# Routing tokens to experts: rows of x written straight to the experts' order, with token number and gate, instead of a routing table in DRAM

## The chip, the cores and the metric

The kernel runs on one core of a Trainium2 chip. The metric is the device time of one execution in microseconds (us). The core has five engines that run side by side, each with its own in-order list of instructions: TensorE (PE; its weight loads are PEld), VectorE (DVE), ScalarE (ACT), GpSimd (POOL) and SyncE (SP), which here only issues DMAs. TensorE has two clock levels, 1.2 and 2.4 GHz; the profile gives the granted clock as a share of full speed.

## The reference

```python
def _attn_ref(r, k, v, w, u):                 # batch 4, 8 heads, 768 steps, head size 48
    for t in range(S):
        cur = einsum('bhd,bhe->bhde', u * kt, vt)
        y[:, :, t] = einsum('bhd,bhde->bhe', rt, state + cur)
        state = w * state + einsum('bhd,bhe->bhde', kt, vt)

def _moe_ref(x, w_gate, w1, w2, capacity):    # 3072 tokens x 384, 8 experts of 384 -> 1024 -> 384
    expert_idx = argmax(x @ w_gate, axis=1)
    gate_w = softmax(x @ w_gate)[arange(N), expert_idx]
    # each expert takes its tokens in token order, at most capacity (768) of them
    h = maximum(einsum('ecd,edf->ecf', disp, w1), 0)
    y = einsum('ecf,efd->ecd', h, w2)
    out[i] = gate_w[i] * y[expert_idx[i], pos[i]]      # kept tokens, the others are zero
```

The output of the attention, with the heads side by side, is the x of the experts.

## The kernel before

**Attention loop.** The 3072 tokens are 24 tiles of 128. The loop over the tiles is written out as a hand-made software pipeline: iteration i issues, in this order, the loads of tile i+5 (`load`, on SP's and ACT's queues), the bonus products of tile i+3 (`bonus`, two GpSimd products), the scores of tile i+1 (`scores` on TensorE, `masks` on VectorE), the diagonals of tile i+2 (`diag`, ACT), the back projection of tile i-1 (`back_out`), then `values` and `update` of tile i on TensorE, a step of the routing (`advance`), `prep_keys`, the state update (`state_of`) and `prep_values` (its `reduce_bonus`, L450, is the VectorE sum that waits for the bonus products), and at its end up to two routing scatters (`scatters(2)`). Each engine runs its own share of that order.

**Routing.** `back_out` turns the attention result of a tile into token-major x in PSUM, together with the gate logits; ACT copies x to SBUF (L505) and SP writes it to the DRAM tensor `x_dr` (L506). Tiles are routed in groups of four, at the end of two: `route` finds each token's expert, adds to the running counts per lane (`lane`, L105, on GpSimd but for the last group), ranks the tokens by two small matmuls (L112 and L113), and makes a `slot` (expert * 3072 + rank) and a gate per token. The pair (token number, gate) of each token stands in `pay`. An indirect DMA per tile (`scatters`, L133) writes 128 pairs of 8 bytes to the DRAM table `tbl` at their slots. In iteration 2 GpSimd has filled that table with a number out of bounds.

**Experts.** There are nine passes: expert 0 twice (its first 160 places, then 256 more), each other expert once with 416 places. Before a pass SP reads the pass's part of the table back into `ids` (`table`, L213), and GpSimd gathers the rows of x by the token numbers in it with four indirect DMAs (`gather`, L222); numbers out of bounds are skipped. Then come the transposes (`xtrans`, L231), two layers of fp32 products in three parts each (`layer1`, `layer2`), transposes back and a scatter to the output (`finish`, `emit`, L283 and L275), scaled by the gate from `ids`.

**The order around the change.** Pass 0 needs tokens of the first 16 tiles only: its table is read at iteration 19 and its rows are gathered at iterations 21 and 22 (two gathers each, called a to d in the prediction) from the first 2048 rows of `x_dr`, beside the loop. After the loop come its transposes, the back projection and routing of the last tile, layer 1, the last scatters, and after four blocks of layer 1 the tables of pass 1 and of all later passes and the gathers of passes 1 and 2. From pass 1 on the gather of pass k+2 is issued at the start of pass k. Scatters among themselves are declared independent; any other pair of a write and a read of the same DRAM tensor by indirect DMA is ordered by a wait.

Of the kernel before, what the change touches and what calls it, by code (L numbers as in the profile page):

```python
# [18 lines left out]
C = 128  # L19
NC = S // C  # L20
NI = B * NC
# [4 lines left out]
OOB = 1 << 30  # L26
# [8 lines left out]
def rwkv_moe(nc, tc, dmj, rkv, bdc, wv, uv, ub, wg, w1, w2, out, cap):  # L35
# [4 lines left out]
    with ExitStack() as ctx:  # L40
# [3 lines left out]
        tbl = dram.tile([E * NT, 2], I32, name="tbl")  # L44
# [6 lines left out]
        pay = const.tile([128, NI, 2], I32, name="pay")  # L51
        oob = const.tile([128, E * NT * 2 // 128], I32, name="oob")
# [17 lines left out]
        def back(i, xs, sm, ps1, nd=None):  # L70
            gi, i0, n = grp[i]
            if i == i0:
                lsum[gi] = sm.tile([128, n, E], F32, tag="l", name=f"l{gi}")
            xp = ps1.tile([128, NP, 96 + E], F32, tag="xp", name=f"xp{i}")
            for p in range(NP):
                nc.tensor.matmul(xp[:, p], lhsT=xs[:, p], rhs=sel[:, p], start=True, stop=True)
            nc.vector.tensor_reduce(out=lsum[gi][:, i - i0], in_=xp[:, :, 96:].rearrange("p a e -> p e a"), axis=AX.X, op=ALU.add)
            if i == i0 + n - 1:
                routing.append(route(gi, i0, n, lsum.pop(gi), sm, ps1, nd))
            return xp  # L80
# [7 lines left out]
        def route(gi, i0, n, l, sm, ps1, nd):  # L88
# [37 lines left out]
            nc.vector.reciprocal(out=pay[:, i0:i0 + n, 1].bitcast(F32), in_=zs)  # L126
            todo.extend((i, nd) for i in range(i0, i0 + n))
# [3 lines left out]
        def scatters(n):  # L131
            for i, nd in todo[:n]:
# [6 lines left out]
        def flags(sm, ps1):  # L139
# [4 lines left out]
            cs = sm.tile([128, E + 2], F32, tag="cs", name="cs")  # L144
            nc.vector.tensor_copy(out=cs, in_=ct)
            ff = sm.tile([128, E + 4], F32, tag="ff", name="ff")
# [14 lines left out]
        with ExitStack() as mc:  # L161
# [9 lines left out]
            xg = [keep.tile([WL // 4, 4, DM], F32, name=f"xg{j}") for j in range(2)]  # L171
# [36 lines left out]
            def table(k, rows):  # L208
                e, s0, _, _ = PASSES[k]
                q = max(PASSES[j][2] for j in rows)  # L210
                n = len(rows)
                t = keep.tile([q, n, 4, 2], I32, name=f"ids{k}")
                nc.sync.dma_start(out=t.rearrange("p e i t -> p e (i t)"),  # L213
                                  in_=tbl.rearrange("(e n) t -> e (n t)", e=E)[e:e + n, 2 * s0:2 * s0 + 8 * q]
                                  .rearrange("e (p k) -> p e k", k=8))
                for j, kk_ in enumerate(rows):
                    ids[kk_] = t[:, j]

            def gather(k, n=NT, part=range(4)):
# [52 lines left out]
            def emit(k, i, yp, qo):  # L272
                yo = mo.tile([qo, DM], F32, tag="yo", name=f"yo{k}_{i}")
                nc.scalar.mul(out=yo, in_=yp, mul=ids[k][:qo, i, 1:2].bitcast(F32))  # L274
                r = nc.gpsimd.indirect_dma_start(out=out[:, :], out_offset=bass.IndirectOffsetOnAxis(ap=ids[k][:qo, i, 0:1], axis=0),  # L275
# [30 lines left out]
            sb = [wk.tile([128, 2, NP, 128], F32, name=f"s{j}", bufs=1) for j in range(3)]  # L306
            snb = [wk.tile([128, NP, 64], F32, name=f"snb{j}", bufs=1) for j in range(2)]
# [55 lines left out]
            def setup3():  # L363
# [17 lines left out]
            wz = oob.bitcast(BF16)[:, 0:512]  # L381
# [160 lines left out]
            for i in range(NI):  # L542
# [33 lines left out]
            yt = buf.tile([128, 3, WL], F32, name="yt")  # L576
            for j in range(3):
# [9 lines left out]
            scatters(NI)  # L587
            act()
# [14 lines left out]
            table(1, [1])  # L603
            table(2, list(range(2, len(PASSES))))
# [222 lines left out]
```

## Time and profile before

| | us |
|---|---|
| median of 3 runs | 454.87 |
| lowest and highest | 452.69, 457.9 |
| profiled execution | 453.87 |
| its span, first to last instruction | 452.1 |
| TensorE busy in the span | 390.6 (86%) |
| VectorE, ScalarE, GpSimd busy | 257.6, 201.3, 184.8 |

The profile gives for each engine how long it was busy, for each line of the kernel how long its instructions took and what ended the idle time before them (`[4.42 <-POOL lane L105]`: idle for 4.42 us until GpSimd's instruction of line 105 was done), and for each DMA the time from issue to landing. A busy engine in one stage says nothing of another: the loop over the tiles ends near 172 us, the passes over the experts follow.

### The profile page before, as it was taken

To read this page: it belongs to the slowest core of one execution; us is meant where nothing else is said; L and a number is where in the kernel's file an instruction comes from. 1 tells how busy PE (TensorE), PEld (TensorE's weight loads), DVE (VectorE), ACT (ScalarE), POOL (GpSimd) and SP (SyncE) were. 2 spreads that over 40 slices of the span, in tenths; PEclk is the share of its full clock that TensorE was granted. 3 is DMA by queue.
4 is the path that set the end of the run, shared out by engine and by line. 5 is a ranking of instruction groups with operands and counts; after the bars stand their busy time and mean duration, and the time that the engine had idled before them with its cause. 6 is when DMAs were issued, how large, how long until landed. Compare 5 with 4: busy or idle time off the path is not lost.

```text
span 452.1 us, 8646 instructions
## 1 busy us (share of the span) xinstructions
PE 390.6 (86%) x3234; PEld 364.9 (81%) x3235; DVE 257.6 (57%) x527; ACT 201.3 (45%) x502; POOL 184.8 (41%) x224
## 2 busy tenths in 40 slices
PE   4599868798977587949999999999999999999950
PEld 1489657687866477939999999999999999999940
DVE  6799897887687354815545464553654545543100
ACT  2577546575453233516455273462643634524020
POOL 5765784978366352247440330423303301103030
PEclk8589997896798858987999999999999999999995
DMA  8899999999996252863734553554545534301020
GB/s 220 227 237 280 289 139 219 183 188 216 156 246 108 29 99 45 100 178 111 220 105 132 158 150 123 158 154 146 151 127 170 160 96 129 112 0 50 2 61 1
DMA packets 24871, 64.18 MB, mean 142 GB/s; under 512 B 6575, under 2 KB 9991, under 8 KB 24821
## 3 DMA queue, kind: packets, MB, share of 16 engines
q1 hardware_dynamic: 18101, 49.01, 43.8%
q0 software_dynamic: 5184, 9.82, 8.0%
q10 hardware_dynamic: 1536, 4.72, 5.5%
q8 instruction: 27, 0.44, 0.5%
q14 instruction: 23, 0.19, 0.2%
HBM read 54.26 MB, written 10.05 MB: 142 GB/s over the span
## 4 chain that ended last, share of the span: by engine, by line
PE 30%; issue 20%; POOL 4%; DMA 1%; POOLq 0%
PE a L250 5%; PE a L248 5%; PE a L249 5%; PE b L267 4%; PE b L269 4%; PE b L268 4%; POOL out L275 3%; PE yp L283 2%; PE tp L231 1%; POOL xg L222 1%; DMA xg<-x_dr,ids 1%; DMA tbl<-pay,slot 0%; POOLq L771 0%; POOLq L275 0%; POOLq L222 0%
## 5 line engine op out<-in xcount | busy, mean ns | idle before, releaser
L427 ACT ACTIVATE s<-eye,bon 128x128 f32<-128x128 f32 x192 | 58.7, 388 | 58.2 <-DVE bon L450 57.6
L275 POOL DMA_INDIRECT out<-yo,ids x36 | 36.0, 1001 | 105.2 <-ACT yo L274 104.0
L248 PE MATMUL a<-xh,ws 128*128 128x416 f32 (+1 forms) x216 | 76.8, 355 | 0.0
L249 PE MATMUL a<-xl,ws 128*128 128x416 f32 (+1 forms) x216 | 73.8, 342 | 0.0
L250 PE MATMUL a<-xh,ws 128*128 128x416 f32 (+1 forms) x216 | 73.8, 341 | 0.0
L267 PE MATMUL b<-hh,ws 128*128 128x416 f32 (+2 forms) x216 | 73.3, 339 | 0.0
L269 PE MATMUL b<-hh,ws 128*128 128x416 f32 (+2 forms) x216 | 71.6, 331 | 0.0
L268 PE MATMUL b<-hl,ws 128*128 128x416 f32 (+2 forms) x216 | 71.3, 330 | 0.0
L222 POOL DMA_INDIRECT xg<-x_dr,ids x36 | 38.0, 1056 | 79.5 <-PE tp L231 57.5
L195 DVE TENSOR_TENSOR ws<-wr,ws 128x384 fp32r<-128x384 f32 (+1 forms) x110 | 66.3, 620 | 6.9 <-ACT ws L193 6.7
L254 DVE SCALAR_TENSOR_TENSOR hl<-a,hh 128x416 fp32r<-128x416 f32 (+1 forms) x72 | 39.8, 553 | 51.0 <-ACT hh L253 50.7
L253 ACT ACTIVATE hh<-a 128x416 fp32r<-128x416 f32 (+1 forms) x72 | 35.2, 489 | 73.6 <-PE a L250 73.3
L193 ACT CAST ws<-wr 128x384 fp32r<-128x384 f32 (+1 forms) x112 | 59.8, 556 | 6.0 <-DMA wr<-w 6.0
L270 DVE COPY yt<-b 128x416 f32<-128x416 f32 (+2 forms) x27 | 14.6, 542 | 66.3 <-PE b L269 66.3
L458 PEld LDWEIGHTS a<-dm 48*128 48x128 f32 x384 | 27.6, 214 | 20.7 <-DVE s L462 12.7
L458 PE MATMUL a<-dm 48*128 48x128 f32 x384 | 32.9, 314 | 13.0 <-DVE s L462 7.2
L248 PEld LDWEIGHTS a<-xh,ws 128*128 128x128 f32 x216 | 42.3, 196 | 0.5
L249 PEld LDWEIGHTS a<-xl,ws 128*128 128x128 f32 x216 | 42.2, 195 | 0.3
L250 PEld LDWEIGHTS a<-xh,ws 128*128 128x128 f32 x216 | 42.0, 195 | 0.2
L268 PEld LDWEIGHTS b<-hl,ws 128*128 128x128 f32 x216 | 40.7, 189 | 0.3
L267 PEld LDWEIGHTS b<-hh,ws 128*128 128x128 f32 x216 | 40.7, 189 | 0.2
L269 PEld LDWEIGHTS b<-hh,ws 128*128 128x128 f32 x216 | 40.5, 188 | 0.3
(133 smaller groups left out, 614.1 us busy)
## 6 DMA issues: line engine op xcount, KB each, us to landing
bd<-bdc SPq DMA_DIRECT2D x24, 576.0 KB, 8.0
wr<-w SPq DMA_DIRECT2D x24, 512.0 KB, 5.2
wr<-w SPq DMA_DIRECT2D x32, 384.0 KB, 3.4
dm<-dmj ACTq DMA_DIRECT2D x24, 192.0 KB, 9.0
dm<-dmj SPq DMA_DIRECT2D x24, 192.0 KB, 6.5
x_dr<-x SPq DMA_DIRECT2D x24, 192.0 KB, 5.4
xg<-x_dr,ids POOLq DMA_INDIRECT x36, 4.3
out<-yo,ids POOLq DMA_INDIRECT x36, 4.1
```

The source lines that it names most:

```text
L193: nc.scalar.copy(out=hi, in_=r)
L195: eng.tensor_tensor(out=lo, in0=r, in1=hi.bitcast(F32), op=ALU.subtract)
L222: nc.gpsimd.indirect_dma_start(out=xg[k % 2][:q, i], out_offset=None, in_=x_dr[:n, :], in_offset=bass.IndirectOffsetOnAxis(ap=ids[k][:q, i ...
L248: nc.tensor.matmul(a, lhsT=wh, rhs=xh[:, d, :n], start=d == 0, stop=False)
L249: nc.tensor.matmul(a, lhsT=wh, rhs=xl[:, d, :n], start=False, stop=False)
L250: nc.tensor.matmul(a, lhsT=wl, rhs=xh[:, d, :n], start=False, stop=d == 2)
L267: nc.tensor.matmul(o, lhsT=wh, rhs=hh[:, f, :n], start=f == 0, stop=False)
L268: nc.tensor.matmul(o, lhsT=wh, rhs=hl[:, f, :n], start=False, stop=False)
L269: nc.tensor.matmul(o, lhsT=wl, rhs=hh[:, f, :n], start=False, stop=f == 7)
L275: r = nc.gpsimd.indirect_dma_start(out=out[:, :], out_offset=bass.IndirectOffsetOnAxis(ap=ids[k][:qo, i, 0:1], axis=0), in_=yo, in_offset= ...
L427: nc.scalar.mul(out=s[:, h, p], in_=eye, mul=t["bon"][:, 2 * p + h:2 * p + h + 1])
L458: nc.tensor.matmul(a[:, h, p], lhsT=t["dm"][r, 1, p], rhs=t["dm"][r, 0, p], start=True, stop=True)
```

## The change

Each tile's row of x, 384 numbers, gets two more columns, the token number (as a float) and the gate, in a row of 400 (1600 bytes). The scatter writes that whole row at the token's slot of a new DRAM tensor `xsd`, already in the experts' order. The write of x to `x_dr` by SP, the table, its fill and its read-back fall away. Three row buffers `xr` of four tiles each stand in SBUF.

Where an expert's rows lie is then known without a table: place p of an expert is read if p lies below the expert's end, which is the count of its tokens. `counts` (the count matmuls that the flags needed anyway) is moved ahead, and `places` makes from it a penalty and an index for each place of all later passes; `early_places` does so for pass 0 from the counts after 16 tiles. `gather` reads by these indices; `take` then turns the two extra columns of the gathered rows into output indices and gates, ahead of each pass's transposes. The gather of pass 1 now follows the last scatters directly. The branches that run only for unusual inputs are rewritten to match (left out below).

```diff
@@ back: the copy of x goes into the row buffer
+            xr = rows(gi)
             if i == i0:
                 lsum[gi] = sm.tile([128, n, E], F32, tag="l", name=f"l{gi}")
+                nc.scalar.copy(out=xr[:, 0:n, DM], in_=idf[:, i0:i0 + n])
...
-            return xp
+            nc.scalar.copy(out=xr[:, i - i0, 0:DM].rearrange("p (a b) -> p a b", a=NP), in_=xp[:, :, 0:96])
@@ route, scatters
-            nc.vector.reciprocal(out=pay[:, i0:i0 + n, 1].bitcast(F32), in_=zs)
-            todo.extend((i, nd) for i in range(i0, i0 + n))
+            nc.vector.reciprocal(out=xr[:, 0:n, DM + 1], in_=zs)
+            todo.extend((i, xr[:, i - i0], nd) for i in range(i0, i0 + n))
...
-                r = nc.gpsimd.indirect_dma_start(out=tbl[:, :], out_offset=bass.IndirectOffsetOnAxis(ap=slot[:, i:i + 1], axis=0),
-                                                 in_=pay[:, i], in_offset=None, bounds_check=E * NT - 1, oob_is_err=False)
+                r = nc.gpsimd.indirect_dma_start(out=xsd[:, :], out_offset=bass.IndirectOffsetOnAxis(ap=slot[:, i:i + 1], axis=0),
+                                                 in_=row.bitcast(I32), in_offset=None, bounds_check=E * NT - 1, oob_is_err=False)
@@ new
+        def places(k, n, end, sm):
+            sh = [128, n, 4]
...
+            nc.vector.tensor_tensor(out=pen[:, k:k + n], in0=pos[:, k:k + n], in1=end.unsqueeze(2).broadcast_to(sh), op=ALU.is_ge)
+            nc.vector.scalar_tensor_tensor(out=pidx[:, k:k + n], in0=pen[:, k:k + n], scalar=FAR, in1=pos[:, k:k + n],
+                                           op0=ALU.mult, op1=ALU.add)
+
+        def early_places(sm, ps1):
+            ct = ps1.tile([128, 1], F32, tag="lg", name="ct0")
+            nc.tensor.matmul(ct, lhsT=ones, rhs=lane[:, SNAP, 0:1], start=True, stop=True)
+            places(0, 1, ct, sm)
@@ table falls away; gather, take
-                    nc.gpsimd.indirect_dma_start(out=xg[k % 2][:q, i], out_offset=None, in_=x_dr[:n, :],
-                                                 in_offset=bass.IndirectOffsetOnAxis(ap=ids[k][:q, i, 0:1], axis=0),
-                                                 bounds_check=n - 1, oob_is_err=False)
+                    nc.gpsimd.indirect_dma_start(out=xg[k % 2][:q, i].bitcast(I32), out_offset=None, in_=xsd[:, :],
+                                                 in_offset=bass.IndirectOffsetOnAxis(ap=pidx[:q, k, i:i + 1], axis=0),
+                                                 bounds_check=E * NT - 1, oob_is_err=False)
+
+            def take(k):
+                q = PASSES[k][2]
+                t = keep.tile([WL // 4, 4], I32, tag="ids", name=f"ids{k}", bufs=2)
+                g = keep.tile([WL // 4, 4], F32, tag="gw", name=f"gw{k}", bufs=2)
+                nc.vector.scalar_tensor_tensor(out=t[:q], in0=pen[:q, k], scalar=FAR, in1=xg[k % 2][:q, :, DM], op0=ALU.mult, op1=ALU.add)
+                nc.vector.tensor_copy(out=g[:q], in_=xg[k % 2][:q, :, DM + 1])
+                ids[k] = t, g
@@ setup on GpSimd
-                nc.gpsimd.iota(pay[:, :, 0], pattern=[[C, NI]], base=0, channel_multiplier=1)
-
-            def setup4():
-                nc.gpsimd.memset(oob, OOB)
-                nc.gpsimd.dma_start(out=tbl.rearrange("(p n) t -> p (n t)", p=128), in_=oob)
+                ii = sup.tile([128, NI], I32, name="ii")
+                nc.gpsimd.iota(ii, pattern=[[C, NI]], base=0, channel_multiplier=1)
+                nc.gpsimd.tensor_copy(out=idf, in_=ii)
+                ip = sup.tile([128, len(PASSES), 4], I32, name="ip")
+                for k, (e, s0, _, q) in enumerate(PASSES):
+                    nc.gpsimd.iota(ip[:, k], pattern=[[q, 4]], base=e * NT + s0, channel_multiplier=1)
+                nc.gpsimd.tensor_copy(out=pos, in_=ip)
+                for t in xrb:
+                    nc.gpsimd.memset(t[:, :, DM:], 0.0)
@@ back_out
-                xp = back(i, T[i]["xs"], sm, ps1, "tbl")
-                x = wk.tile([128, DM], F32, tag="x", name=f"x{i}")
-                nc.scalar.copy(out=x.rearrange("p (a b) -> p a b", a=NP), in_=xp[:, :, 0:96])
-                nc.sync.dma_start(out=x_dr[C * i:C * i + C, :], in_=x)
+                back(i, T[i]["xs"], sm, ps1, lambda g: xrb[g % 3], "rows")
@@ the loop over the tiles
                 if i == 19:
-                    table(0, [0])
+                    early_places(sm, ps1)
                 if i in (21, 22):
-                    gather(0, C * SNAP, ((0, 1), (2, 3))[i - 21])
-                if i == 2:
-                    setup4()
+                    gather(0, ((0, 1), (2, 3))[i - 21])
@@ after the loop
+            take(0)
             for j in range(3):
                 xtrans(0, j)()
...
             scatters(NI)
+            counts(ps1)
+            places(1, E, cs[:, 0:E], sm)
+            gather(1)
             act()
...
-            table(1, [1])
-            table(2, list(range(2, len(PASSES))))
-            gather(1)
             gather(2)
...
+            take(1)
             for d in range(3):
                 xtrans(1, d)()
...
                 if k + 1 < len(PASSES):
+                    take(k + 1)
```

## Rows read from the trace of the kernel before

**Rows 1.** The busy time of each engine by stage: the stretch in us, its length, then busy us (and instructions) of PE, PEld, DVE, ACT and POOL, the granted TensorE clock as a share of full speed, the DMA engines' busy share, and GB/s.

```profile
140.00:160.00 20.00, 12.38 (x184) 10.91 (x184) 10.45 (x30) 7.58 (x25) 8.41 (x10) 0.84 0.38 41
...
180.00:200.00 20.00, 15.69 (x134) 15.27 (x132) 11.82 (x37) 7.51 (x19) 6.00 (x7) 1.00 0.77 145
200.00:210.00 10.00, 7.36 (x37) 6.41 (x37) 2.39 (x5) 3.16 (x7) 7.83 (x8) 0.50 0.29 85
...
220.00:437.00 217.00, 215.69 (x1257) 210.73 (x1256) 101.79 (x186) 92.29 (x192) 52.85 (x52) 1.00 0.40 118
```

**Rows 2.** The chain of waits that ended last, in order of time: start, us, what.

```profile
183.66 0.97 DMA tbl<-pay,slot
184.64 12.37 issue
...
201.01 2.68 DMA xg<-x_dr,ids
203.73 1.22 PE tp L231 x9
```

**Rows 3.** The timeline of TensorE, 140 to 210 us: start, us, line, operation, output and inputs, shapes, count, and in brackets the idle time before it and what ended that.

```profile
148.06 1.16 PE L458 MATMUL a<-dm 48*128 48x128 f32 x16
...
157.99 0.17 PE L113 MATMUL rk<-lane,ones 128*128 128x16 bf16 x1 [4.42 <-POOL lane L105]
159.64 2.08 PE L458 MATMUL a<-dm 48*128 48x128 f32 x16 [1.48 <-DVE s L462]
...
174.56 0.94 PE L231 MATMUL tp<-idn,xg 64*128 64x64 f32 x10 [2.30 <-DMA xg<-x_dr,ids]
...
195.41 0.28 PE L269 MATMUL b<-hh,ws 128*128 128x256 f32 x1
200.63 0.37 PE L231 MATMUL tp<-idn,xg 64*128 64x64 f32 x1 [4.94 <-DMA xg<-x_dr,ids]
...
203.73 1.22 PE L231 MATMUL tp<-idn,xg 64*128 64x64 f32 x9 [0.86 <-DMA xg<-x_dr,ids]
```

**Rows 4.** The timeline of SP's DMA queue in the same stretch: the two times at which the routing table is read back.

```profile
149.58 0.54 SPq L213 DMA_DIRECT2D ids<-tbl  x1
...
192.17 1.15 SPq L213 DMA_DIRECT2D ids<-tbl  x2
```

**Rows 5.** The timeline of GpSimd, 140 to 205 us; an indirect DMA's time here is that of its issue, not of its landing.

```profile
153.38 1.01 POOL L133 DMA_INDIRECT tbl<-pay,slot  x1 [10.05 <-DMA ids<-tbl]
...
167.89 0.96 POOL L222 DMA_INDIRECT xg<-x_dr,ids  x1 [0.30 <-issue]
...
183.66 0.97 POOL L133 DMA_INDIRECT tbl<-pay,slot  x1 [0.30 <-issue]
197.22 0.97 POOL L222 DMA_INDIRECT xg<-x_dr,ids  x1 [12.59 <-issue]
...
201.01 0.94 POOL L222 DMA_INDIRECT xg<-x_dr,ids  x1 [0.30 <-issue]
```

**Rows 6.** The timeline of VectorE in the same stretch: the last instruction of a group's gates (L126) and one long wait.

```profile
143.66 0.17 DVE L126 RECIPROCAL pay<-zs 128x2 f32<-128x2 f32 x1
...
157.81 0.55 DVE L450 TENSOR_REDUCE bon<-t 128x8 f32<-128x384 f32 x1 [7.02 <-POOL t L420]
...
162.24 0.17 DVE L126 RECIPROCAL pay<-zs 128x2 f32<-128x2 f32 x1
```

**Rows 7.** Lines of the kernel that issue DMAs: the routing scatter (L133), the final scatter (L275) and the write of x (L506), each with the time of an issue in ns (min/median/max) and, in the row below it, the time from issue to landing of that line's DMAs; the last row is the landing of the gathers (L222).

```profile
L133 POOL DMA_INDIRECT tbl<-pay,slot x24: 975/1002/2344, 52.1 to 183.7; - x24
...
DMA to landing us min/median/max: 6.7/13.9/17.6
L275 POOL DMA_INDIRECT out<-yo,ids x36: 906/996/1314, 207.8 to 436.7; - x36
...
DMA to landing us min/median/max: 2.8/4.1/5.0
L506 SPq DMA_DIRECT2D x_dr<-x x24: 332/347/739, 30.9 to 177.8; - x24
...
DMA to landing us min/median/max: 2.6/5.4/14.2
DMA to landing us min/median/max: 3.2/4.3/5.3
```

**Rows 8.** The busy time by stretches of 4 us in the loop, columns as in rows 1: one in which the first routing scatters are only being issued (from 52) and two that follow the issue of such scatters (from 60 and from 112).

```profile
52.00:56.00 4.00, 3.45 (x64) 3.05 (x65) 4.00 (x6) 2.13 (x8) 3.61 (x3) 1.00 1.04 303
...
60.00:64.00 4.00, 3.04 (x48) 2.55 (x44) 3.96 (x4) 3.33 (x10) 3.70 (x3) 1.00 0.90 81
...
112.00:116.00 4.00, 4.00 (x33) 3.47 (x34) 2.10 (x3) 1.24 (x4) 1.49 (x2) 0.50 0.86 77
```

**Rows 9.** Of the timeline of GpSimd the first bonus product and one that waited for a load, and of ACT's one of its shortest instructions; then of the lists of waits between 20 and 140 us one of GpSimd and the first of VectorE (who waited for whom: us in total, times, longest).

```profile
9.87 1.15 POOL L419 TENSOR_TENSOR t<-bd,ubt 128x384 f32<-128x384 f32 x1 [3.91 <-DMA bd<-bdc]
...
31.51 1.37 POOL L419 TENSOR_TENSOR t<-bd,ubt 128x384 f32<-128x384 f32 x1 [3.10 <-DMA bd<-bdc]
...
161.59 0.22 ACT L109 ACTIVATE z<-z 128x16 f32<-128x16 f32 x1
...
POOL t L419 <- DMA bd<-bdc: 8.1, 3, 3.1
...
DVE ws L195 <- ACT ws L193: 4.9, 4, 3.4
```

More of the change, by code (lines that the diff above doesn't have):

```diff
@@ L43, in rwkv_moe @@
         x_dr = dram.tile([NT, DM], F32, name="x_dr")
-        tbl = dram.tile([E * NT, 2], I32, name="tbl")
+        xsd = dram.tile([E * NT, XW], I32, name="xsd")
+        ebd = dram.tile([2, E], F32, name="ebd")
         idn = const.tile([128, 128], F32, name="idn")
@@ L143, in flags @@
             nc.tensor.matmul(ct[:, E + 1:], lhsT=ones, rhs=lane[:, SNAP, 0:1], start=True, stop=True)
-            cs = sm.tile([128, E + 2], F32, tag="cs", name="cs")
             nc.vector.tensor_copy(out=cs, in_=ct)
+        def places(k, n, end, sm):
+            sh = [128, n, 4]
+            if clamp:
+                c = sm.tile([128, n], F32, tag="cl", name=f"cl{k}")
+                nc.vector.tensor_tensor(out=c, in0=end, in1=top[:, 0:n], op=ALU.min)
+                end = c
+            nc.vector.tensor_tensor(out=pen[:, k:k + n], in0=pos[:, k:k + n], in1=end.unsqueeze(2).broadcast_to(sh), op=ALU.is_ge)
[5 more added lines that the diff above has]
+            places(0, 1, ct, sm)
+        def flags(sm):
             ff = sm.tile([128, E + 4], F32, tag="ff", name="ff")
@@ L170, in rwkv_moe @@
             mc.enter_context(tc.manual_schedule())
-            xg = [keep.tile([WL // 4, 4, DM], F32, name=f"xg{j}") for j in range(2)]
+            xg = [keep.tile([WL // 4, 4, XW], F32, name=f"xg{j}") for j in range(2)]
             wtiles = {}
@@ L206, in rwkv_moe, with gather @@
             ids = {}
[L208 to L219, printed above, removed]
+            def gather(k, part=range(4)):
                 q = PASSES[k][2]
                 for i in part:
-                    nc.gpsimd.indirect_dma_start(out=xg[k % 2][:q, i], out_offset=None, in_=x_dr[:n, :],
-                                                 in_offset=bass.IndirectOffsetOnAxis(ap=ids[k][:q, i, 0:1], axis=0),
-                                                 bounds_check=n - 1, oob_is_err=False)
+                    nc.gpsimd.indirect_dma_start(out=xg[k % 2][:q, i].bitcast(I32), out_offset=None, in_=xsd[:, :],
[8 more added lines that the diff above has]
+                ids[k] = t, g
             def xtrans(k, j):
@@ L306, in rwkv_moe @@
             sb = [wk.tile([128, 2, NP, 128], F32, name=f"s{j}", bufs=1) for j in range(3)]
+            xrb = [wk.tile([128, 4, XW], F32, name=f"xr{j}", bufs=1) for j in range(3)]
             snb = [wk.tile([128, NP, 64], F32, name=f"snb{j}", bufs=1) for j in range(2)]
@@ L380, in rwkv_moe @@
                 nc.sync.dma_start(out=wp[64 * h:64 * h + D], in_=wv[D * h:D * h + D])
-            wz = oob.bitcast(BF16)[:, 0:512]
+            wz = sup.tile([128, 512], BF16, name="wz")
             nc.vector.memset(wz, 0.0)
@@ L687, in reroute, with row_tile @@
         def reroute():
-            nc.gpsimd.dma_start(out=tbl.rearrange("(p n) t -> p (n t)", p=128), in_=oob)
             with tc.tile_pool(name="rw", bufs=2) as rw, tc.tile_pool(name="rs", bufs=2) as rs, \
                     tc.tile_pool(name="rp", bufs=1, space=PSUM) as rp:
+                rows = {}
+                def row_tile(g):
+                    if g not in rows:
+                        rows[g] = rw.tile([128, 4, XW], F32, tag="xr", name=f"rr{g}")
+                        nc.vector.memset(rows[g], 0.0)
+                    return rows[g]
                 for i in range(NI):
@@ L699, in reroute, with ends @@
                     nc.scalar.copy(out=xs, in_=tp)
-                    back(i, xs, rs, rp)
+                    back(i, xs, rs, rp, row_tile)
                     advance()
                     advance()
-                scatters(NI)
-                flags(rs, rp)
+                    scatters(NI)
+                counts(rp)
+                flags(rs)
+                ends()
+        def ends():
+            nc.sync.dma_start(out=ebd[0:1], in_=top[0:1])
+            nc.sync.dma_start(out=ebd[1:2], in_=cs[0:1, 0:E])
         def window(e, s0, n):
@@ L708, in window @@
             with tc.tile_pool(name="vw", bufs=1) as vw, tc.tile_pool(name="vp", bufs=2, space=PSUM) as vp:
-                di = vw.tile([q, 4, 2], I32, name="di")
-                nc.sync.dma_start(out=di.rearrange("p i t -> p (i t)"),
-                                  in_=tbl.rearrange("(e n) t -> e (n t)", e=E)[bass.ds(e, 1), 2 * s0:2 * (s0 + n)]
-                                  .rearrange("o (p k) -> (o p) k", k=8))
+                eb = vw.tile([q, 2], F32, name="eb")
+                for j in range(2):
+                    nc.sync.dma_start(out=eb[:, j:j + 1], in_=ebd[j:j + 1, bass.ds(e, 1)].broadcast_to([q, 1]))
+                wi = vw.tile([q, 4], I32, name="wi")
+                nc.gpsimd.iota(wi, pattern=[[q, 4]], base=s0 - min(cap, NT), channel_multiplier=1)
+                wp_ = vw.tile([q, 4], F32, name="wp_")
+                nc.vector.tensor_copy(out=wp_, in_=wi)
+                nc.vector.tensor_scalar(out=wp_, in0=wp_, scalar1=eb[:, 0:1], scalar2=None, op0=ALU.add)
+                en = vw.tile([q, 1], F32, name="en")
+                nc.vector.tensor_tensor(out=en, in0=eb[:, 0:1], in1=eb[:, 1:2], op=ALU.min)
+                wn = vw.tile([q, 4], F32, name="wn")
+                nc.vector.tensor_scalar(out=wn, in0=wp_, scalar1=en, scalar2=FAR, op0=ALU.is_ge, op1=ALU.mult)
+                nc.vector.tensor_tensor(out=wi, in0=wn, in1=wp_, op=ALU.add)
                 a1 = vw.tile([128, 3, F], F32, name="a1_")
```

46 lines of the change are left out of this document (25 added, 21 removed).

## The prediction, made before the changed kernel was run

> **What bounds the kernel now.** Read the stages first [rows 1]. From 220 us on TensorE is busy 215.69 of 217.00 us at granted clock 1.00: nothing but TensorE work counts there, and the change takes none of it away. Before that there are holes: TensorE works only 15.69 of 20 us in 180 to 200, and 7.36 of 10 us at clock 0.50 in 200 to 210. The chain of waits names the second hole [rows 2]: the last routing scatter is issued at 183.66, a nameless 12.37 us follow, then come the gather of pass 1 and its transposes at 203.73. TensorE's own line agrees [rows 3]: its last matmul of pass 0 starts at 195.41, the transposes wait 4.94 us and again piecemeal until 203.73, and the next matmuls run slow until 210. SP's line says what the 12.37 us are [rows 4]: the read-back of the routing table is issued only at 192.17, when the scatter of 183.66 has landed, 8.5 us after its issue; the gather follows at 197.22 [rows 5], after one more DMA trip.
>
> GpSimd's line shows a first hole [rows 5]. The scatter of tile 16 was ready at about 143.8, when DVE had its gates [rows 6], but started at 153.38 after 10.05 us of waiting: it may not overwrite the table while SP's read of it, issued at 149.58 [rows 4], is under way. Queued behind it is the bonus of tile 23, so DVE stands 7.02 us for it [rows 6], and TensorE 4.42 us for the lane sums behind that [rows 3]. TensorE then runs at 0.50: sixteen score matmuls take 2.08 us at 159.64 against 1.16 at 148.06 [rows 3].
>
> The profiled execution has 452.1 us of span and 453.87 in all; the shown runs have a median of 454.87 (452.69 to 457.9). I sum against 453.87, so the forecast may sit 1 us low against the median.
>
> **The unknown: how long a scatter of whole rows takes to land (L).** After the change every gather waits for the scatters ahead of it, so L sets the result. 8-byte rows took 6.7/13.9/17.6 us (min/median/max); scatters of 1536-byte rows from the same queue at the end of a pass 2.8/4.1/5.0; plain writes of x 2.6/5.4/14.2 [rows 7]. Slow landing goes with tiny rows, not with load alone: where such scatters are in flight the DMA engines are as busy (shares 0.90, 0.86) but move 81 and 77 GB/s, against a share of 1.04 and 303 GB/s just as the first of them are issued [rows 8]. The new rows are 1600 bytes, nearest to the out scatter in queue, operation and size, and nearest to the x write in bytes (128 rows). I take 4.5, between 4.1 and 5.4, and keep 2.8 and 13.9 as ends. The Trainium skill (DMA: Bandwidth & Descriptors, "Anatomy of one DMA") gives about 2.0 us plus bytes over 436 GB/s, an estimate of 2.5 us for 205 KB; the steps below would then end near 434. No row for such a transfer is that short on average, so I stay with the rows.
>
> **First hole.** The table read goes; at iteration 19 stand one small matmul and two DVE operations instead (0.17 us each, as the short ones in [rows 6]). So scatters 16 and 17 go at 144.0 and 145.3 (1.3 apart, as the gathers from 197.22 to 201.01 [rows 5]), the bonus follows, DVE does not stand, and its gates of tiles 18 and 19 come at 155.7 instead of 162.4 (7.02 less, some of it lost to the small operations). TensorE asked for the data of the transposes of pass 0 at 172.3 (174.56 less its wait of 2.30 [rows 3]). Less 7.0, and less 0.9 for each of some three groups of matmuls that ran at 0.50 as the one at 159.64 did, it now asks at about 162.7. But those need gathers that now sit in one queue with scatters and wait for them in both directions, since both touch the same DRAM tensor:
> - scatter 17 lands at 145.3 + 4.5 = 149.8; gathers a and b go at 149.8 and 151.1, land (4.3 [rows 7]) at 155.4;
> - scatters 18 and 19 need that and their gates: 155.7 and 157.0; land at 161.5;
> - gathers c and d: 161.5 and 162.8; land at 167.1.
> Before, gather d was issued at 167.89 [rows 5] and the transposes resumed at 174.56 [rows 3]. So the transposes are 7.4 us earlier; 4.4 of the 11.8 us that TensorE had won turn into a new wait. What GpSimd holds behind those waits, the lane sums of tiles 20 and 21, comes near 159, before TensorE asks at 162.6.
>
> **Second hole.** Scatter 23 went 9.1 us after the transposes (183.66 against 174.56), so now at 176.2, and lands at 180.7. Counts and indices (three matmuls, three DVE operations of 0.17) are ready before, under that landing; should a landing of 2.8 not cover them, they cost 0.5. Four gathers at 180.7 to 184.5 (at the same spacing); the last took 2.7 us then [rows 2], at the median 4.3: landed by 187.2 to 188.8. TensorE ends pass 0 at 195.7 - 7.4 = 188.3. So the transposes of pass 1, whose last part started at 203.73, start at 188.8: 14.9 us gained in all, the 7.4 among them, and almost no wait left. Without the long idle time the 5.2 us from 204.9 to 210.1 at 0.50 [rows 1, 3] become 2.6: another 2.6.
>
> **The rest.** 24 x writes leave SP's queue, where each waited for ACT's copy; the weight and input loads behind them can only go earlier. The fill of the table leaves GpSimd. About 14 short index operations join its setup, at most 2 us, while its first bonus product waits 3.91 us for a load [rows 9]: free, and up to 2 us if that load came at once. ACT gets 8 short copies (the shortest ACT row is 0.22 [rows 9]), and each pass two DVE operations ahead of its transposes. In the last stage DVE is busy 101.79 of 217.00 us [rows 1]; they wait for a gather issued a whole pass earlier, so TensorE does not see them. I charge 0.5 for all this. Moving 4.7 MB from SP's hardware queue to GpSimd's costs GpSimd no more issues: 24 before, 24 after, 1002 ns each at the median [rows 7].
>
> **Sum.** 14.9 + 2.6 - 0.5 = 17.0; 453.87 - 17.0 = 436.9, so 437.
>
> **Rivals.**
> 1. *The landing is set by the software queue, not by row size.* Then L stays at 8.5, as seen from 183.66 to 192.17, or somewhat above. For L above 4.8 each link lengthens: gather d lands at 157.8 + 2L, scatter 23 goes at 166.9 + 2L, pass 1 is there at 173.7 + 3L. L = 8.5 gives 199.2, a gain of 4.5: 449.4; at L = 10.0 nothing is gained: 454. The change would then not shorten what it sets out to. For it: the scatters of tiny and of long rows have 128 rows each, and some issues stretch to 2344 ns [rows 7]. Against it: the out scatters, at 104 rows, are never above 5.0. The Trainium skill (SBUF — State Buffer, "SBUF: two separate sides") warns that DMAs issued from GpSimd wait for descriptors while DVE holds a shared port, which speaks against moving x there; of it this trace shows that stretch of issue time alone. Chance 0.13.
> 2. *Slower: the two-way waits become the bound.* The same chain at L = 13.9, the median of the tiny scatters, puts pass 1 at 215.4, 11.7 later than 203.7: 466. It decides from L = 10.0 on; below that the trip to the table costs more. For it: x writes themselves reached 14.2 under load. Against it: that load is the loop's, and after 140 the DMA share falls to 0.38 [rows 1]. Chance 0.07.
> 3. *The loop gets faster too.* If loads pace it, freeing the DMA engines of tiny rows pays before 140. GpSimd waits 8.1 us for loads between 20 and 140 [rows 9], 3.10 of it at 31.51, before the first scatter; the other 5.0 on top of the sum give 432, and with TensorE's clock kept up in the loop perhaps 428. Against it: DVE's waits there, the longest group of which is 4.9 us behind ACT's weight casts [rows 9], name no load. Chance 0.15.
>
> **How the numbers follow.** The forecast has 0.65: its own spread is L = 2.8 to 6.7, 435 to 444 (at 2.8 TensorE's own work sets the start of pass 1, at 186.6; at 6.7 pass 1 is there at 193.8, a gain of 9.9). The range adds rival 3 below and half of the way to rival 1 above: 428 to 448; it leaves out rivals 1 and 2, 0.20. A measurement of this kernel can tell about 1%, 4.5 us. Faster by over 1%: forecast and rival 3, 0.80. Within 1%: rival 1, 0.13. Slower: rival 2, 0.07.
>
> **What would show it.** In the changed kernel's rows: scatters of whole rows landing in 4 to 5 us; no GpSimd wait of 10 us near 143 and no 7 us wait of DVE; a GpSimd wait of some 4 us ahead of gathers a and c; TensorE's wait at the transposes of pass 0 grown from 2.3 to about 4 us, that of pass 1 shrunk from 8 to under 2; clock 1.00 after it; the span from the last transpose of pass 1 to the end unchanged near 247 us but for the clock. The prediction falls if scatters land in over 7 us, if the loop before 140 changes by more than 3 us either way, or if some wait of the new row buffers shows up in ACT.

## The result and the profile after

The changed kernel takes 435.72 us (median of 4 runs, 434.58 to 439.62) against 455.5 us for the kernel before (median of 4 runs): a ratio of 0.9583 [0.9501, 0.9665], 4.2% faster, where 437.0 was forecast. The profiled execution took 436.04 us, with a span of 434.3 us against 452.1: 17.8 us less, where the sum gave 17.0.

The busy time by stage of the changed kernel, columns as in [rows 1]:

```profile
140.00:160.00 20.00, 16.39 (x208) 14.55 (x209) 15.13 (x41) 8.18 (x25) 10.33 (x13) 0.83 0.16 54
160.00:180.00 20.00, 18.18 (x159) 17.10 (x159) 13.13 (x54) 9.82 (x26) 8.50 (x9) 0.91 0.44 145
180.00:200.00 20.00, 18.74 (x152) 18.32 (x151) 12.01 (x26) 10.12 (x26) 15.43 (x16) 0.91 0.54 160
200.00:210.00 10.00, 10.00 (x86) 9.99 (x85) 4.72 (x12) 2.72 (x7) 3.77 (x4) 1.00 0.61 206
```

The two holes are filled: TensorE works 16.39 us of 140 to 160 (12.38 before) and all of 200 to 210 (7.36 at clock 0.50 before). Its timeline shows both sets of transposes, which answer to those of [rows 3]:

```profile
162.52 0.33 PE L251 MATMUL tp<-idn,xg 64*128 64x64 f32 x2
163.19 0.27 PE L251 MATMUL tp<-idn,xg 64*128 64x64 f32 x1 [0.33 <-DMA xg<-xsd,pidx]
164.33 0.77 PE L251 MATMUL tp<-idn,xg 64*128 64x64 f32 x9 [0.87 <-DMA xg<-xsd,pidx]
...
185.78 0.40 PE L251 MATMUL tp<-idn,xg 64*128 64x64 f32 x3
187.43 0.77 PE L251 MATMUL tp<-idn,xg 64*128 64x64 f32 x9 [1.26 <-DMA xg<-xsd,pidx]
...
190.12 0.41 PE L269 MATMUL a<-xl,ws 128*128 128x256 f32 x1
...
193.52 0.28 PE L268 MATMUL a<-xh,ws 128*128 128x256 f32 x1
```

Pass 0 is transposed at 164.33 instead of 174.56, 10.2 us earlier; pass 1 at 187.43 instead of 203.73, 16.3 us earlier. The rest of the 17.8 us lies behind that, in the clock: matmuls of layer 1 run slow (0.41 us each instead of 0.28) from 189 to 192.4 here, and from 204.9 to 210.1 before.

GpSimd's timeline, which answers to [rows 5]: scatters 16 and 23 (L140) and the gathers (L234) that open each group.

```profile
141.32 1.25 POOL L140 DMA_INDIRECT xsd<-xr,slot  x1 [1.00 <-DVE xr L133]
...
149.43 1.01 POOL L234 DMA_INDIRECT xg<-xsd,pidx  x1 [0.62 <-issue]
...
155.72 1.02 POOL L140 DMA_INDIRECT xsd<-xr,slot  x1 [4.02 <-DVE snb L508]
...
160.37 0.97 POOL L234 DMA_INDIRECT xg<-xsd,pidx  x1 [1.80 <-DMA xsd<-xr,slot]
...
173.53 0.98 POOL L140 DMA_INDIRECT xsd<-xr,slot  x1 [0.31 <-issue]
179.38 0.96 POOL L234 DMA_INDIRECT xg<-xsd,pidx  x1 [4.87 <-DVE ff L181]
```

The wait of 10.05 us at scatter 16 has become 1.00. From the last scatter to the first gather of pass 1 it takes 5.9 us instead of 13.6. The scatters' line and the landing of its DMAs answer to [rows 7]:

```profile
L140 POOL DMA_INDIRECT xsd<-xr,slot x24: 974/1004/1864, 52.5 to 173.5; - x24
...
DMA to landing us min/median/max: 2.6/3.9/6.0
```

The stretches of 4 us answer to [rows 8]. In them the DMA engines move 294 and 194 GB/s, not 81 and 77. In the first, whole rows are in flight; in the second they may have landed already, as their scatters were issued by 108.5 and landed 3.9 us later at the median:

```profile
60.00:64.00 4.00, 2.81 (x45) 2.39 (x40) 2.57 (x5) 2.69 (x8) 3.91 (x4) 1.00 0.97 294
...
112.00:116.00 4.00, 3.21 (x46) 2.75 (x44) 3.90 (x6) 0.18 (x2) 2.86 (x3) 1.00 0.67 194
```

So the number came out as forecast. Open was which part of the change brings it: that the trip to the table is gone, that the write of x is gone, or that no scatter writes 8-byte rows any more. The theory of the forecast credited the trip and the row length together. The rivals tested: the tiny rows alone do it; or the trip alone does.

### The profile page after: what moved, and what is told of

Its sections match the earlier page's. It is cut to its first block, busy times and chain, and to the rows that moved or that the text cites. A ratio compares the mean times of both kernels' runs of the same rounds, so it can differ in the third digit from the quotient of the medians.

```text
span 434.3 us, 8672 instructions
## 1 busy us (share of the span) xinstructions
PE 383.4 (88%) x3235; PEld 359.7 (83%) x3236; DVE 260.1 (60%) x549; ACT 201.5 (46%) x510; POOL 183.9 (42%) x236
## 4 chain that ended last, share of the span: by engine, by line
PE 54%; DVE 14%; issue 14%; ACT 7%; POOL 3%; DMA 3%; ACTq 0%; POOLq 0%; DVEq 0%; SPq 0%
PE a L268 7%; PE a L270 7%; PE a L269 7%; PE b L287 6%; PE b L288 6%; PE b L289 6%; ACT s L452 4%; PE y L522 3%; PE y L518 3%; DVE dm L462 3%; PE a L483 2%; PE yp L303 2%; POOL out L295 2%; PE tp L251 2%; PE xp L83 2%
## 5 line engine op out<-in xcount | busy, mean ns | idle before, releaser
L234 POOL DMA_INDIRECT xg<-xsd,pidx x36 | 38.2, 1062 | 72.8 <-PE tp L251 56.9
```

## The experiments

**The changed kernel again.** No edit; it gives the spread of one execution.

> The changed kernel as it is, run again beside the variants. If its first profile was typical: ratio to the kernel before 0.955 to 0.965 (435 to 438 us), the last routing scatter landing in 5 to 6 us, and tile 20's masks some 3 us earlier than in the kernel before (136 against 139 us). If those 3 us in the loop were chance of one execution, they differ by over 2 us here.

It took 436.98 us (435.88 to 437.41), ratio 0.958 [0.9519, 0.964], with transposes at 164.70 and 188.30 against 164.33 and 187.43. Two executions of one kernel differ by about 1 us at such a point. The masks of tile 20 start at 137.80 here, against 136.10 and 139.07 in the kernel before: over half of the 3 us in the loop was chance of one execution.

**A second scatter beside the first, of 8 bytes or of 1600 bytes.** Both kernels do work that the reference doesn't need: each scatter of a tile is followed by another to a tensor `side` that nobody reads.

```diff
+        side = dram.tile([E * NT, 2], I32, name="side")        # 1600 bytes: [E * NT, XW]
...
+                    r = nc.gpsimd.indirect_dma_start(out=side[:, :], out_offset=bass.IndirectOffsetOnAxis(ap=slot[:, i:i + 1], axis=0),
+                                                     in_=row[:, DM:DM + 2].bitcast(I32), ...)   # 1600 bytes: in_=row
```

> The changed kernel, and behind each routing scatter a second one that writes token number and gate, 8 bytes a row, to a side tensor that nobody reads (work that the reference doesn't need). Theory (tiny rows block the DMA engines): row scatters land late again, in over 8 us at the median instead of 3.9, the loop loses its 3 us, and through the two-way waits of scatters and gathers (3 times the added landing, less the slack) pass 1 starts 10 to 15 us later: 446 to 452 us. Rival (landing goes by the number of rows in GpSimd's queue): the same as the next run's, whatever that is. Each second scatter costs GpSimd 1.3 us more in both runs.

> The same with whole rows of 1600 bytes to the side tensor, so 200 times the bytes of the run before, and the same number of rows and issues. Theory (tiny rows block the DMA engines): row scatters land in 4 to 6 us at the median, the loop loses 0 to 2 us, the whole 1 to 5 us: 437 to 441. Rival (number of rows): over 8 us to landing and 446 to 452, as with 8 bytes. A second rival (bytes decide): slower than the run with 8 bytes.

8 bytes: 464.73 us (463.03 to 465.45), ratio 1.0181 [1.0115, 1.0247]. 1600 bytes: 456.49 us (453.04 to 458.42), ratio 0.9977 [0.994, 1.0014]. Both lie far above what was expected. 24 more scatters on GpSimd, each an issue of about 1.0 us and 0.3 us of gap, cost some 19.5 us in the second kernel (456.49 - 436.98). The loop's bonus products stand behind them in GpSimd's list, and VectorE now waits for these (from the list of waits of the second kernel, 20 to 215 us):

```profile
DVE bon L479 <- POOL t L449: 11.8, 5, 4.3
```

How much of the 19.5 us is the issues alone, and how much the 4.9 MB that these rows write, the run doesn't separate. What tells the two kernels apart is the difference: 200 times the bytes are 8.2 us cheaper. The landing of the kernel's own row scatters, first with 8-byte company, then with 1600-byte company:

```profile
DMA to landing us min/median/max: 5.2/7.4/11.7
```

```profile
DMA to landing us min/median/max: 2.6/5.2/7.8
```

Over 8 us at the median was expected beside 8-byte rows, 7.4 came. Tiny rows slow the transfers beside them too. This speaks for the row length, but in both kernels the scatters that the gathers wait for still have whole rows, and 24 more issues stand beside them, so it does not settle the question.

**The write of x put back.** After each `back`, SP again writes the tile of x to `x_dr`, which nobody reads.

```diff
                 back(i, T[i]["xs"], sm, ps1, lambda g: xrb[g % 3], "rows")
+                gi, i0, _ = grp[i]
+                nc.sync.dma_start(out=x_dr[C * i:C * i + C, :], in_=xrb[gi % 3][:, i - i0, 0:DM])
```

> The changed kernel with the 24 writes of x from SP's queue put back (to a tensor that nobody reads; work that the reference doesn't need). Theory (the loop gained by the tiny rows alone): tile 20's masks within 1 us of the changed kernel's 136, the whole within 1 us of it. Rival (the loop gained because SP's queue no longer waits for the copies of x, or by 4.7 MB less in that queue): the 3 us are lost again, 438 to 440 us.

437.5 us (437.23 to 437.75), ratio 0.9597 [0.9538, 0.9655]: no difference from the changed kernel. The masks of tile 20 start at 137.11. The writes that left SP's queue were worth nothing that can be seen.

**The trip put back, before pass 1 and at iteration 19.** SP reads token numbers and gates of some rows back. In the first kernel GpSimd copies them before the gathers of pass 1, so that these wait for the trip; in the second the read stands where the table was read in the loop, and holds up the scatters behind it only by the order of write and read.

```diff
-            gather(1)
...
+            nc.sync.dma_start(out=rb[0], in_=xsd[EARLY:EARLY + 128, DM:DM + 2].rearrange("(p k) t -> p k t", k=4))
+            nc.gpsimd.tensor_copy(out=rb[1], in_=rb[0])
+            gather(1)
             gather(2)
```

```diff
                 if i == 19:
                     early_places(sm, ps1)
+                    rb = keep.tile([40, 4, 2], I32, name="rb")
+                    nc.sync.dma_start(out=rb, in_=xsd[0:EARLY, DM:DM + 2].rearrange("(p k) t -> p k t", k=4))
```

> The changed kernel with a read-back put in where the old table was read: SP reads token numbers and gates of 128 places of pass 1 from the new tensor, GpSimd copies them, and only then gathers pass 1 (work that the reference doesn't need; the gathers still use the indices from the counts). Theory: the trip costs what SP's trip showed before, some 3 us to land and under 1 us around it, all of it seen by TensorE at the transposes of pass 1, whose wait grows from 1.3 to about 5 us: the whole 3.5 to 5 us slower than the changed kernel. Rival (all of the second hole was the slow landing of tiny rows): under 1.5 us.

> The changed kernel with one read-back by SP at iteration 19 put in, of pass 0's 160 token numbers and gates; nobody uses it, but scatters 16 and 17 must wait until it is done (work that the reference doesn't need). Theory (the first hole was a short read behind a slow landing): with scatters that land in 4 us GpSimd waits some 3 to 4 us instead of 10.05, VectorE's wait for the bonus products stays under 2 us instead of 7.02, and the whole is 0 to 2 us slower than the changed kernel. Rival (the read-back itself makes the hole): GpSimd waits 8 us or more, 5 to 7 us slower.

Before pass 1: 439.46 us (435.74 to 440.33), ratio 0.9672 [0.9591, 0.9753]. GpSimd's timeline of that kernel:

```profile
174.89 0.98 POOL L140 DMA_INDIRECT xsd<-xr,slot  x1 [0.30 <-issue]
182.60 0.70 POOL L628 COPY rb<-rb 32x8 int32<-32x8 int32 x1 [6.73 <-DMA rb<-xsd]
183.47 0.99 POOL L234 DMA_INDIRECT xg<-xsd,pidx  x1 [0.16 <-DVE ws L218]
```

The gather follows the last scatter by 8.6 us instead of 5.9: the trip costs 2.7 us there, where some 4 were expected. TensorE's waits at the transposes of pass 1 add up to 2.9 us, not the 5 expected. In the whole it is at most some 1%, and the interval overlaps that of the changed kernel. SP issued its read 5.6 us after the scatter (at 180.48), so the landing of the last scatters takes most of the 5.9.

At iteration 19: 434.08 us (432.78 to 437.56), ratio 0.9591 [0.9508, 0.9673], nothing lost. GpSimd's timeline there, and SP's read of the same kernel:

```profile
138.12 0.99 POOL L140 DMA_INDIRECT xsd<-xr,slot  x1 [0.30 <-issue]
...
143.72 1.01 POOL L140 DMA_INDIRECT xsd<-xr,slot  x1 [2.51 <-DVE kt L468]
...
140.75 0.90 SPq L584 DMA_DIRECT2D rb<-xsd  x1
```

The read-back stands in the same place as in the kernel before, yet scatter 16 waits 2.51 us, not 10.05, and no VectorE sum waits behind it. In the kernel before the wait has two parts. It begins at 143.33, and scatter 15 went at

```profile
140.22 0.98 POOL L133 DMA_INDIRECT tbl<-pay,slot  x1 [0.30 <-issue]
```

Until 149.58 SP can't even issue its read [rows 4]: 6.3 of the 10.05 us are the landing of the tiny scatters that the read waits for. The last 3.8 us are the read itself. Here SP issues its read 2.6 us after scatter 15, and scatter 16 goes 3.0 us after that read and 2.3 us after its gates (ready at 141.45). So the read does hold GpSimd, but briefly, and TensorE doesn't see it.

**The kernel before with longer table rows.** The decisive one: table, read-back, gathers by token number and the write of x all stay; only the rows of the table grow from 8 bytes to 64 and to 512, of which 8 are used. The table is filled and read back expert by expert, since its rows no longer fit one fill; the same kernel with rows of 8 bytes is the control for that.

```diff
-        tbl = dram.tile([E * NT, 2], I32, name="tbl")
+        tbl = dram.tile([E * NT, TW], I32, name="tbl")         # TW = 2, 16, 128
...
-            pay = const.tile([128, NI, 2], I32, name="pay")
+            pay = const.tile([128, NI, TW], I32, name="pay")
...
-                nc.sync.dma_start(out=t.rearrange("p e i t -> p e (i t)"), ...)
+                for j in range(n):
+                    a = (e + j) * NT + s0
+                    nc.sync.dma_start(out=t[:, j], in_=tbl[a:a + 4 * q, 0:2].rearrange("(p k) t -> p k t", k=4))
```

> The kernel before with its table filled and read back expert by expert (8 fills of 416 places, one read per pass) and rows of 8 bytes as before: the control for the next two. Both theories: 452 to 458 us; scatters land in 10 to 16 us at the median; the loop's tile 20 is masked at 137.5 to 141 us (139.07 in the kernel before; 136.1 to 139.5 in seven runs with whole rows).

> The same with rows of 64 bytes in the table, of which only 8 are used and read back: as many rows and issues, eight times the bytes. Theory (a row's size decides): the landing is shorter than 8-byte rows' only if the loss ends below 64 bytes; I expect over 8 us still and 450 to 457 us. Rival (number of rows): as the control.

> The same with rows of 512 bytes, of which only 8 are used and read back: as many rows and issues, 64 times the bytes; table, read-back, writes of x and the order are those of the kernel before. Theory (a row's size decides): scatters land in 3 to 6 us at the median, GpSimd's wait at iteration 19 falls from 10 to about 5 us and VectorE's behind it from 7.0 to under 2, the last read-back comes 5 to 6 us after the last scatter instead of 8.5: 443 to 448 us. Rival (number of rows in GpSimd's queue): over 10 us to landing, 452 to 458.

| table rows | us (lowest to highest) | ratio to the kernel before |
|---|---|---|
| 8 bytes (control) | 459.11 (456.61 to 459.57) | 1.0119 [1.0051, 1.0187] |
| 64 bytes | 437.81 (434.08 to 438.94) | 0.9662 [0.9599, 0.9725] |
| 512 bytes | 440.24 (438.99 to 442.41) | 0.9736 [0.9671, 0.9802] |

My expectation was wrong here: I held that 64 bytes would recover little and that the trip would keep its price. A table with 64-byte rows brings 3.4% of the 4.2%, and the two intervals overlap. Against the control, which fills and reads the table in the same way, it is 21.3 us faster, 4.6%; the control itself came out 1.2% slower than the kernel before, so the 3.4% may be too low for the row length alone. The landing of the routing scatters, for 8, 64 and 512 bytes:

```profile
DMA to landing us min/median/max: 5.3/9.1/13.6
```

```profile
DMA to landing us min/median/max: 2.1/4.0/7.2
```

```profile
DMA to landing us min/median/max: 2.3/4.9/5.6
```

The busy time of the stretch 40 to 140 us (columns as in [rows 1]), first with 8-byte, then with 64-byte table rows:

```profile
40.00:140.00 100.00, 80.28 (x1106) 70.24 (x1102) 87.01 (x160) 54.75 (x164) 69.26 (x66) 0.91 0.97 207
```

```profile
40.00:140.00 100.00, 83.02 (x1150) 72.83 (x1146) 88.13 (x164) 57.05 (x171) 72.90 (x68) 0.91 0.71 210
```

At the same rate, 207 and 210 GB/s, the DMA engines are busy 0.97 of the time with 8-byte rows and 0.71 with 64-byte rows. And what became of the waits, from the timelines of GpSimd, SP and TensorE (us; a dash where there is no such read; the profiled execution of the 64-byte kernel, 434.08 us, is the fastest of its five runs):

| | scatter 15 to the read at iteration 19 | idle before scatter 16 | scatter 23 to the first gather of pass 1 | transposes of pass 0, pass 1 |
|---|---|---|---|---|
| kernel before | 9.4 | 10.05 | 13.6 | 174.56, 203.73 |
| table, 8 bytes | 11.8 | 11.52 | 13.6 | 176.28, 209.74 |
| table, 64 bytes | 2.7 | 3.33 | 7.0 | 162.96, 185.51 |
| table, 512 bytes | 2.7 | 3.36 | 7.2 | 168.36, 189.97 |
| changed kernel | - | 1.00 | 5.9 | 164.33, 187.43 |

The lines of GpSimd and SP behind the second and third columns, first 8 bytes (scatter 16, SP's read), then 64 bytes (scatters 15 and 16, SP's read):

```profile
154.89 1.01 POOL L138 DMA_INDIRECT tbl<-pay,slot  x1 [11.52 <-DMA ids<-tbl]
...
152.09 0.54 SPq L220 DMA_DIRECT2D ids<-tbl  x1
```

```profile
137.95 0.98 POOL L138 DMA_INDIRECT tbl<-pay,slot  x1 [0.30 <-issue]
...
144.37 1.01 POOL L138 DMA_INDIRECT tbl<-pay,slot  x1 [3.33 <-DVE bon L456]
...
140.67 0.61 SPq L220 DMA_DIRECT2D ids<-tbl  x1
```

The lines of GpSimd behind the fourth column, first 8 bytes, then 64 bytes, with SP's read of the latter:

```profile
186.31 1.13 POOL L138 DMA_INDIRECT tbl<-pay,slot  x1 [0.30 <-issue]
199.92 0.96 POOL L227 DMA_INDIRECT xg<-x_dr,ids  x1 [12.48 <-issue]
```

```profile
170.57 0.97 POOL L138 DMA_INDIRECT tbl<-pay,slot  x1 [0.30 <-issue]
...
177.60 1.20 POOL L227 DMA_INDIRECT xg<-x_dr,ids  x1 [6.06 <-issue]
...
174.76 7.07 SPq L220 DMA_DIRECT2D ids<-tbl  x8
```

With the trip to the table still in it, 13.6 us become 7.0; without the trip they are 5.9. The row length does most of it. The trip itself is more than the 1.1 us between the two: from SP's read to the gather it takes 2.8 us with 64-byte rows (5.1 in the kernel before), but there the last scatter has landed 4.2 us after its issue, against up to 5.9 in the changed kernel. In the Trainium skill, DMA: Bandwidth & Descriptors, section Specifications, a transfer needs 512 bytes or more for line rate, and a smaller one is done as a read-modify-write. No run shows what happens in the memory, and here the loss ended far below that bound: 64-byte rows land as fast as 512-byte rows. The measurement decides. The 512-byte kernel does its transposes 5.4 us later than the 64-byte one, its loop being later by as much; its eight fills of 208 KB stand in that loop, but whether they are the cause was not tried.

**Further steps on the changed kernel.** The gathers of pass 0 all at iteration 20 (first); with that, two blocks of layer-2 output work ahead of the transposes of pass 1 (second); with both, three buffers instead of two for `ids` and `gw` (third).

```diff
-                if i in (21, 22):
-                    gather(0, ((0, 1), (2, 3))[i - 21])
+                if i == 20:
+                    gather(0)
```

```diff
+            finish(0, 0)
+            finish(0, 1)
             take(1)
             for d in range(3):
                 xtrans(1, d)()
-            finish(0, 0)
-            finish(0, 1)
```

```diff
-  tag="ids", name=f"ids{k}", bufs=2        (and "gw")
+  tag="ids", name=f"ids{k}", bufs=3
```

> The changed kernel with all four gathers of pass 0 at iteration 20, ahead of scatters 18 and 19, instead of two at 21 and two at 22. Theory (the rest of the wait at the transposes of pass 0 is gathers c and d waiting for scatters 18 and 19): that wait goes from 1.2 us to none, and the whole is 1 to 2 us faster than the changed kernel. Rival (scatters 18 to 21 now wait longer for the gathers, and pass 1 with them): no change within 0.5 us, or slower.

> The run before, and the two transposes back of pass 0 (finish 0 and 1) moved ahead of the transposes of pass 1, into TensorE's wait there. Theory: 0.8 us of that wait is filled, and if the clock's fall to 0.50 behind it (3.7 us long in the changed kernel) comes from that idle time, it goes or shrinks, for another 1 to 2 us: 2 to 4 us faster than the changed kernel in all. Rival (the clock falls anyway): at most 1 us on top of the run before.

> The run with all four early gathers at iteration 20 and the transposes back of pass 0 moved ahead, and besides three buffers instead of two for the output indices and gates of a pass, so that VectorE's step ahead of pass 2 does not wait for the output scatters of pass 0. Theory: VectorE's wait of 3.4 to 5.8 us there goes, and the 1.5 to 1.7 us for which TensorE stood behind it in the two runs with early gathers: 1 to 2 us faster than those (433 to 434). Rival (that wait is hidden): no change.

434.59 us (431.81 to 436.38), ratio 0.9576 [0.9517, 0.9635]; 435.44 (431.1 to 437.45), 0.959 [0.9523, 0.9656]; 432.27 (430.34 to 433.81), 0.9555 [0.9507, 0.9603]. Expected were 1 to 2 and 2 to 4 us less than the changed kernel, and for the third 1 to 2 us less than the first two. The first two move waits without shortening the whole: the transposes of pass 0 no longer wait, but then TensorE stands behind VectorE, and VectorE behind a wait that the change brought. `take(2)` writes the buffer of indices that the output scatters of pass 0 still read. From the lists of waits, first a line of the changed kernel, then two of the second step:

```profile
DVE ids L242 <- DMA out<-yo,ids: 3.4, 1, 3.4
```

```profile
DVE ids L242 <- DMA out<-yo,ids: 5.8, 1, 5.8
```

```profile
PE tp L251 <- DVE xl L256: 1.7, 1, 1.7
```

With three buffers both waits are gone and the granted clock of stretches of 10 us is 1.00 from 150 to 220. It has the lowest ratio to the kernel before; against the changed kernel its gain lies inside the intervals.

## Why the prediction was right, and where it was not

- **The number and its place**: right. 17.8 us of span against 17.0, none from the last stage. From the transposes of pass 1 to the end it takes 246.9 us, forecast as near 247 (248.4 before). But in the profiled pair 3.0 us are there before 140 already, which the sum did not have. The masks of tile 20, before and after:

```profile
139.07 1.31 DVE L462 COPY_PREDICATED s<-msk,a 128x1024 f32<-128x1024 int32 x1
```

```profile
136.10 1.32 DVE L487 COPY_PREDICATED s<-msk,a 128x1024 f32<-128x1024 int32 x1
```

- **L, the landing of whole rows**: taken as 4.5, measured 2.6/3.9/6.0, and inside the ends of 2.8 and 13.9 but for the minimum. The nearest rows, the output scatters, were the right ones to lean on. The estimate of 2.5 from the Trainium skill's fixed part and rate (DMA: Bandwidth & Descriptors, Anatomy of one DMA) is under the shortest landing seen.
- **First hole**: its size was off. The wait at the transposes of pass 0 was forecast as 4.4 and measured as 0.33 + 0.87 = 1.2; TensorE asked at 162.52, forecast 162.7 (in part by luck, see the next point). The term that failed is the landing of gathers c and d, taken at the median of 4.3: the last one went at 161.64, 1.2 us before its time in the forecast, and its data was used at 164.33, 2.7 later. So 10.2 us were won, not 7.4.
- **When TensorE asks for pass 0**: the sum took 2.7 us for three groups of slow matmuls that would run at full clock. Slow groups came again, only earlier (the second line is the group that took 1.16 and 2.08 in [rows 3]):

```profile
149.20 1.97 PE L518 MATMUL y<-dm,snb 48*64 48x128 f32 x16 [0.52 <-DVE snb L508]
...
153.77 1.67 PE L483 MATMUL a<-dm 48*128 48x128 f32 x16
```

  Against their lengths at full clock such groups cost an estimated 4.3 us from 159.64 on before and 2.8 us from 147.30 on here, so about 1.5 of the 2.7 us came. The 3.0 us from the loop made up for it, less some smaller delays that were not followed: the time is right, two of its terms are not. In the repeat the loop is ahead by 1.3 us and TensorE asks at 162.25.
- **The two-way waits**: forecast as some 4 us ahead of gathers a and c, measured as 0.62 and 1.80. Gather a went at 149.43, forecast 149.8, but not because a scatter landed: scatter 17 went at 142.87, and 3.9 us later is 146.8. GpSimd's lane sums, ahead of it in the list, ran until 148.81. This time is right by luck.

```profile
147.34 1.47 POOL L112 TENSOR_TENSOR lane<-lane,oh 128x8 bf16<-128x8 bf16 x2 [1.38 <-DVE z L114]
```

- **First hole, its cause**: credited to the table read that goes. Wrong for the larger part, as the read put back at iteration 19 costs nothing that can be seen once the rows are long. Of the 10.05 us, 6.3 were the landing of scatters 14 and 15 ahead of the read, 3.8 the read. The prediction read the line of the wait rightly, and stopped one link too early: what the read itself waited for.
- **Second hole**: 16.3 us, forecast 14.9. The 2.8 us that are ahead by then come from the first hole; the link from scatter 23 to the gather was 5.9, forecast 4.5, and takes 1.4 back.
- **Clock behind the second hole**: forecast 2.6, and 1.5 came. The trace shows the matmuls slow for some 3 us again, behind transposes that had waited only 1.26 us; that the clock would stay up was the wrong step. What decides it stays open: in the run with all gathers at iteration 20 the same transposes waited 1.41 us, and the granted clock of the stretches of 10 us from 180 to 220 was 1.00.
- **The rest**: charged at 0.5. One wait was missed, `take(2)` behind the output scatters (3.4 us of VectorE), hidden from TensorE in the changed kernel. No wait for the row buffers shows up in ACT: its copies of x wait 6.6 us in all between 20 and 215, 6.3 before. The x writes, costed at nothing, are worth nothing. A small index operation of VectorE took 1.53 us at 143.38, not 0.17, beside GpSimd's bonus product, and TensorE did not see it.
- **Rival 1** (the software queue sets the landing) fell: the same queue lands in 3.9. **Rival 2** (two-way waits) fell with it: GpSimd idles 4.02 us at scatter 18, of which the gates (VectorE has them at 154.94) explain 3.2, and 1.80 at gather c. **Rival 3** (a faster loop): the masks of tile 20 start at 136.1 instead of 139.1, but over the kernels with whole rows between 136.1 and 139.5; with the DMA share from 40 to 140 us down from 0.97 to 0.73, it is hardly faster, so loads did not pace it.

What stays open: a 64-byte row changes the length of a write and the distance to its neighbour at once, and no run separates the two. And whether dropping the table beats a table with 64-byte rows: the ratios are 0.8% apart, and their intervals overlap.

## What to carry to other kernels

When a chain shows a long wait for a small read-back, follow what that read waits for before crediting the gain to its removal. Scatters of 8-byte rows cost far more here than their bytes; padding the row (from 8 to 64 bytes it brought 3.4%, the full redesign 4.2%) is a trial of a few lines and should come first. On an engine whose list is shared with the loop's work, more indirect DMAs are not free: 24 more scatters of whole rows cost 19.5 us, 0.8 us each.

## What the hardware showed that was not expected

The tiny rows cost other transfers, more than their own queue. Queues of the two table kernels, 8 bytes first (packets, MB, share of 16 engines' span):

```profile
q1 hardware_dynamic: 18179, 49.01, 44.2%
q0 software_dynamic: 5376, 9.65, 7.8%
```

```profile
q1 hardware_dynamic: 20747, 49.01, 39.2%
q0 software_dynamic: 5376, 10.01, 8.0%
```

The queue that carries the scatters (q0) took the same share with either row length. The hardware queue, with the same 49.01 MB and fewer packets, took 44.2% of 457.8 us beside 8-byte rows and 39.2% of 432.4 us beside 64-byte rows: summed over 16 engines 3238 against 2712 us, 526 more. Of the difference in busy time of all queues, some 416 us lie between 40 and 140 us (0.97 against 0.71 of 16 times 100 us), where the tiny writes are under way. So the packets of that queue took longer beside them; why, no run shows.
